# Pooled attention and a feed-forward block on one core: first values pooled by TensorE, five early tiles in float32, some weight shifts on GpSimd, and a new order of the first two chunks

## The chip, the cores and the metric

One core of a Trainium2 chip runs the whole program. The metric is the device time of one execution in microseconds; several executions are timed and the median is given. Engines are named as in the profile: PE (TensorE), PEld (its weight loads), DVE (VectorE), ACT (ScalarE), POOL (GpSimd), SP (the queue that issues nearly all DMAs).

## The reference

```
# q, k, v: [8 batches, 8 heads, 576, 64] float32
k_p = k.reshape(B, H, 72, 8, D).mean(axis=3)          # keys and values pooled by 8
v_p = v.reshape(B, H, 72, 8, D).mean(axis=3)
attn = softmax(q @ k_p^T / 8);  x = attn @ v_p         # -> x: [8, 576, 512]
xn = (x - mean) / sqrt(var + 1e-6) * g_ln              # layer norm over 512
out = x + relu(xn @ w_ch1) @ w_ch2                     # 512 -> 2048 -> 512
```

The two weight matrices arrive as float64 (8 MB each). q, k and v are float32.

## The kernel before

The 4608 rows are 36 tiles of 128, and nine chunks of four tiles. A batch is 576 rows, four and a half tiles, so that some tiles span two batches.

Attention of a tile t has two parts. `stage_a` (token A) loads a later tile's queries, computes the scores on PE in float32 against the pooled keys `kblk` (two buffers, one per batch in turn), subtracts the maximum on DVE, takes the exponential on ACT (`probs`), and brings the probabilities into a form with the keys on the partitions, `pt`. `values` (token B) multiplies by the pooled values, divides by the sum, computes the layer norm, and writes `zT`, the normalized tile transposed, as a float16 high and a float16 low half. For tiles below `XT` (8) the transposes are PE matmuls with an identity, and the split of `pt` into high and low halves is an ACT copy (L311) and a DVE subtract (L312); `values` then takes three float16 matmuls per head (L354). From tile 8 on the halves are made in SBUF on ACT and POOL (L314 to L324), and an SP DMA transposes them (L331, and L416 for z). Those tiles read the values in the split and doubled forms `VA` and `VB`, which ACT's queue copies.

The feed-forward of a chunk c is in three float16 products each way. `ffn_in` (L433) makes the hidden rows, 16 blocks of 128; token I.c.q is a quarter of them, with a third number for half of the columns. The result leaves PSUM by an ACT relu (L441) and a DVE subtract (L442) into a `ring` buffer. `ffn_out` (L462) makes the output rows in two halves of the hidden dimension; token O.c.h is half h for the four tiles. In full a chunk takes 192 matmuls of 512 columns each way.

The weights need work before any of this. Each of 8 blocks of 1 MB a matrix is loaded (token R.mat.b, `load_raw`) into a `raw` buffer (two of them) or, for the first four of w1, a `ring` buffer (four). `convert` (token C.mat.b) makes float32 of float64 by bits: ACT takes the high word (L165), DVE shifts the low word right by 29 (L168) and joins them (L169), and ACT's Abs pass (L177) sums magnitudes. After four blocks, `max_w1` or `max_w2` (M1.h, M2.h) derives a power-of-two scale over all partitions, and `split_w` (S.mat.b) writes the float16 halves, the high one on ACT (L140), the low one on DVE (L141).

Keys and values of later batches are loaded and pooled by adds on POOL (HK.b.i, HV.b.i: halves of a batch; the second HV also does `max_v` and `split_v`). For batch 0, `first_loads` (LD), `first_k` (K0) and `first_v` (V0) do it on DVE and POOL in turns; V0 ends in `max_v` and `split_v`.

The program of the first two chunks is the string `START`, a list of these tokens. It gives instructions their priority; the framework places them on the engines by a simulated timeline, so that an engine's order can differ from the list where an operand or a buffer isn't ready. On the chip each engine runs its own order and waits by semaphores. From chunk 2 on a loop writes the order: the 16 `ffn_in` and 8 `ffn_out` units of a chunk with `stage_a` and `values` of the next chunk between them.

Of the kernel before, what the change touches and what calls it, by code (L numbers as in the profile page):

```python
# [60 lines left out]
def attn_ffn_kernel(ctx: ExitStack, tc: tile.TileContext, qT, kT, v, g, w1, w2, out):  # L61
# [89 lines left out]
    def load_raw(mat, b):  # L151

        raw = ring_tile() if mat == 1 and b < NKT else raw_tile()
        raws[mat, b] = raw = raw.rearrange("p a f c -> p (a f c)").bitcast(I32)
        queue = nc.sync
        queue.dma_start(out=raw, in_=(w1, w2)[mat - 1][b].bitcast(I32))

    def convert(mat, b):
# [6 lines left out]
        nc.scalar.activation(  # L165
            out=w, in_=hi.bitcast(F32), func=AF.Prelu, scale=2.0**-112, alpha=-(2.0**32)
        )
        nc.vector.tensor_single_scalar(out=lo, in_=lo, scalar=29, op=ALU.logical_shift_right)  # L168
        nc.vector.scalar_tensor_tensor(  # L169
            out=w.bitcast(I32),  # L170
            in0=w.bitcast(I32),
            scalar=3,
            in1=lo,
            op0=ALU.logical_shift_left,
            op1=ALU.bitwise_or,
        )
        nc.scalar.activation(  # L177
            out=lo.bitcast(F32), in_=w, func=AF.Abs, accum_out=wm[mat][:, b : b + 1]
        )
# [48 lines left out]
    def pool_v(b, h, eng):  # L228
        if h == 0:
            vp[b] = wk1.tile([KV, H, D], F32, name="vp")  # L230
        vr = vraw.pop((b, h))
        eng.tensor_add(out=vr[:, 0:4, :], in0=vr[:, 0:4, :], in1=vr[:, 4:8, :])  # L232
# [1 line left out]
        eng.tensor_add(out=vp[b][:, h, :], in0=vr[:, 0, :], in1=vr[:, 1, :])  # L234

    def max_v(b):
        m = scalar_tile("mv")
        nc.vector.tensor_reduce(
            out=m[:KV], in_=vp[b], axis=AX.XY, op=ALU.max, apply_absolute_value=True
        )  # L240
# [59 lines left out]
    def probs(t):  # L300
        e, ph = E.pop(t), phl[t % 2]
        nc.scalar.activation(out=e, in_=e, func=AF.Exp, scale=EXP_SCALE)  # L302
        if t < XT:
# [7 lines left out]
            nc.scalar.copy(out=hi, in_=src)  # L311
            nc.vector.tensor_tensor(out=pt[:KV, H:], in0=src, in1=hi, op=ALU.subtract)  # L312
            return
# [19 lines left out]
    def values(t):  # L333

        segs = segments(t)
        if len(segs) == 1:
# [27 lines left out]
        nc.vector.tensor_scalar_mul(out=rs, in0=rs, scalar1=cv)
# [34 lines left out]
        nc.vector.tensor_scalar(  # L399
            out=z, in0=x, scalar1=mv[:, 0:1], scalar2=y, op0=ALU.subtract, op1=ALU.mult  # L400
        )
# [191 lines left out]
```

## Time and profile before

| | |
|---|---|
| Median of 3 runs | 910.19 us (909.65 to 911.42) |
| Span of the profiled execution | 911.2 us, the only time of its own that the page gives; 1.0 above the median |
| PE busy | 841.9 us, 92% |
| DVE busy | 442.5 us, 49% |
| ACT busy | 262.7 us, 29% |
| POOL busy | 237.6 us, 26% |
| Mean granted TensorE clock | 0.972 |
| HBM read, written | 45.09 MB, 9.44 MB |

The page's busy shares are for the whole span. Its forty slices are 22.8 us each, with a digit for tenths of busy time. An idle engine costs only where another waits for it. A row by line gives the line of the kernel, the engine, the operation, the tiles, shape and count, then the total busy time, the mean in ns, and the idle time before it with what ended that.

### The profile page before, as it was taken

The numbers are of one execution on the slowest core, as the hardware profiler recorded it, in microseconds if no ns is written. First come the engines' busy times: TensorE is split into PE (matmuls) and PEld (weight loads), VectorE is DVE, ScalarE is ACT, GpSimd is POOL, SyncE is SP. The second block draws the span as 40 slices with busy tenths as digits, with TensorE's granted clock in tenths as the row PEclk, the third lists the DMA queues.
The fourth block names the chain that finished last, engine by engine and source line by source line (L and its number), as shares of the span: only waits on it lengthen the run. The fifth ranks groups of instructions, "written<-read, shape, count | busy, mean of one in ns | idle before, by whom it ended". The sixth has DMA issues, their size and how long they took to land.

```text
span 911.2 us, 12223 instructions
## 1 busy us (share of the span) xinstructions
PE 841.9 (92%) x4692; PEld 433.7 (48%) x4692; DVE 442.5 (49%) x1038; ACT 262.7 (29%) x506; POOL 237.6 (26%) x390
## 2 busy tenths in 40 slices
PE   2433799999999999999999999999999999999998
PEld 1433685444454444455444544544454445444443
DVE  7978784336273555246424552553254335432121
ACT  2666551315132223132313321231223123211020
POOL 4874423004222761046101630131012001200000
PEclk9965799999999999999999999999999999999999
DMA  8867312103043542335222532233222221310001
GB/s 309 282 224 283 114 44 74 24 1 80 26 116 91 136 117 48 92 99 117 59 70 47 136 71 71 47 91 70 58 59 55 62 59 35 59 46 24 0 1 47
DMA packets 112010, 78.39 MB, mean 86 GB/s; under 512 B 90976, under 2 KB 91984, under 8 KB 109904
## 3 DMA queue, kind: packets, MB, share of 16 engines
q1 hardware_dynamic: 110608, 76.57, 31.2%
q10 hardware_dynamic: 1344, 1.05, 0.5%
q8 instruction: 37, 0.61, 0.3%
q14 instruction: 21, 0.17, 0.1%
HBM read 45.09 MB, written 9.44 MB: 60 GB/s over the span
## 4 chain that ended last, share of the span: by engine, by line
PE 81%; DMA 7%; POOL 5%; DVE 4%; issue 1%; ACT 1%; SPq 0%; POOLq 0%; DVEq 0%; ACTq 0%
PE ps_f L433 38%; PE ps_f L462 37%; DMA kr<-in_kT_dram 3%; PE ps L283 3%; POOL vr L232 2%; DMA raw<-in_w_dram 1%; DMA pt<-phl 1%; POOL kr L218 1%; DMA vr<-in_v_dram 1%; PE ps L356 1%; POOL vr L233 1%; PE ps L357 1%; POOL vp L234 1%; DMA raw<-in_v_dram 1%; DVE w L169 1%
## 5 line engine op out<-in xcount | busy, mean ns | idle before, releaser
L433 PE MATMUL ps_f<-zT,w 128*128 128x512 f16 (+1 forms) x1824 | 384.0, 369 | 0.0
L462 PE MATMUL ps_f<-w,ring 128*128 128x512 f16 x1728 | 378.9, 379 | 0.6 <-DVE ring L442 0.6
L433 PEld LDWEIGHTS <-w 128*128 128x128 f16 x1824 | 177.6, 98 | 187.5 <-issue 0.4
L462 PEld LDWEIGHTS <-ring 128*128 128x128 f16 x1728 | 168.3, 98 | 200.3 <-DVE ring L442 1.1
L442 DVE SCALAR_TENSOR_TENSOR ring<-ps_f,ring 128x512 f16<-128x512 f32 (+1 forms) x152 | 99.8, 659 | 142.6 <-ACT ring L441 139.1
L441 ACT ACTIVATE ring<-ps_f 128x512 f16<-128x512 f32 (+1 forms) x152 | 86.9, 574 | 249.1 <-PE ps_f L433 229.1
L472 DVE SCALAR_TENSOR_TENSOR x<-ps_f,c_out,x 128x512 f32<-128x512 f32 x72 | 53.9, 748 | 196.8 <-PE ps_f L462 192.4
L321 POOL TENSOR_TENSOR phl<-e,phl 128x512 f16<-128x512 f32 x28 | 32.8, 1170 | 252.1 <-ACT phl L314 237.4
L302 ACT ACTIVATE e<-e 128x576 f32<-128x576 f32 x36 | 24.6, 683 | 160.5 <-DVE e L293 151.4
L283 PE MATMUL ps<-kblk,q 128*128 128x144 f32 (+1 forms) x320 | 50.4, 322 | 20.3 <-ACT x L373 9.3
L415 POOL TENSOR_TENSOR hl<-z,hl 128x512 f16<-128x512 f32 x28 | 32.4, 1157 | 115.0 <-ACT hl L414 113.2
L373 ACT ACTIVATE x<-ps,rs 128x64 f32<-128x64 f32 x144 | 33.3, 315 | 100.2 <-DVE x L366 66.5
L283 PEld LDWEIGHTS ps<-kblk,q 128*128 128x128 f32 (+1 forms) x320 | 45.0, 203 | 28.9 <-ACT x L373 9.6
L232 POOL TENSOR_TENSOR vr<-vr 72x256 f32<-72x256 f32 x56 | 44.2, 795 | 34.4 <-DMA vr<-in_v_dram 34.2
L234 POOL TENSOR_TENSOR vp<-vr 72x64 f32<-72x64 f32 x56 | 20.4, 378 | 72.1 <-DVE vb L141 71.7
L218 POOL TENSOR_TENSOR kr<-kr 128x288 f32<-128x288 f32 x29 | 27.9, 966 | 43.2 <-DMA kr<-in_kT_dram 42.8
L377 DVE BATCH_NORM_STATS2 st<-x 128x6 f32<-128x512 f32 x36 | 24.9, 691 | 24.5 <-ACT x L373 24.4
L222 POOL TENSOR_TENSOR kblk<-kr 64x72 f32<-64x72 f32 x58 | 21.1, 364 | 48.3 <-PE ps L283 45.4
L414 ACT CAST hl<-z 128x512 f16<-128x512 f32 x28 | 17.3, 618 | 50.7 <-DVE z L399 47.2
L399 DVE TENSOR_SCALAR z<-x,mv,y 128x512 f32<-128x512 f32 x36 | 30.0, 834 | 2.8 <-DVE y L395 0.5
L292 DVE TENSOR_REDUCE mx<-ps 128x8 f32<-128x576 f32 x36 | 27.0, 750 | 5.0 <-PE ps L283 4.9
L314 ACT CAST phl<-e 128x1024 f16<-128x1024 f32 x28 | 29.2, 1042 | 0.5
(93 smaller groups left out, 539.0 us busy)
## 6 DMA issues: line engine op xcount, KB each, us to landing
raw<-in_w_dram SPq DMA_DIRECT2D x12, 1024.0 KB
q<-in_qT_dram SPq DMA_DIRECT2D x36, 256.0 KB
out_dram<-x SPq DMA_DIRECT2D x36, 256.0 KB
kr<-in_kT_dram SPq DMA_DIRECT2D x30, 288.0 KB
vr<-in_v_dram SPq DMA_DIRECT2D x56, 144.0 KB
ring<-in_w_dram SPq DMA_DIRECT2D x4, 1024.0 KB
raw<-in_v_dram SPq DMA_DIRECT2D x8, 144.0 KB
va<-vh ACTq DMA_DIRECT2D x14, 65.0 KB
```

What stands on the lines that cost most here:

```text
L218: eng.tensor_add(out=kr[:, 0:4, :], in0=kr[:, 0:4, :], in1=kr[:, 4:8, :])
L232: eng.tensor_add(out=vr[:, 0:4, :], in0=vr[:, 0:4, :], in1=vr[:, 4:8, :])
L283: nc.tensor.matmul(ps[r, p // 2, p % 2 * 2 * KV : (p % 2 + 1) * 2 * KV], lhsT=q[:, p, r], rhs=kblk[b % NKB][:, p, :], start=True, stop=True,)
L321: nc.gpsimd.tensor_tensor(out=ph[:, 0, :, KA:P], in0=e[:, :, 0:KA], in1=ph[:, 0, :, 0:KA], op=ALU.subtract)
L373: nc.scalar.activation(out=xh[:, 4 + i, :], in_=px[:, 1, i, 0:D], func=AF.Copy, scale=rs[:, 4 + i : 5 + i])
L399: nc.vector.tensor_scalar(out=z, in0=x, scalar1=mv[:, 0:1], scalar2=y, op0=ALU.subtract, op1=ALU.mult)
L415: nc.gpsimd.tensor_tensor(out=zhl[:, 1, :], in0=z, in1=zhl[:, 0, :], op=ALU.subtract)
L433: nc.tensor.matmul(ps, lhsT=w[:, part, fs], rhs=zT[:, kz, cols], start=(n == 0), stop=(n == 3 * NKT - 1),)
L441: nc.scalar.activation(out=h[:, 0, i, cols], in_=ps, func=AF.Relu)
L442: nc.vector.scalar_tensor_tensor(out=h[:, 1, i, cols], in0=ps, scalar=0.0, in1=h[:, 0, i, cols], op0=ALU.max, op1=ALU.subtract,)
L462: nc.tensor.matmul(ps, lhsT=h[:, part, i, cols], rhs=w[:, wp, j], start=(n == 0), stop=(n == 3 * NFT // 2 - 1),)
L472: nc.vector.scalar_tensor_tensor(out=x, in0=ps, scalar=c_out[:, half : half + 1], in1=x, op0=ALU.mult, op1=ALU.add)
```

## The change

- `XT` goes from 8 to 5. Tiles 0 to 4 keep the PE transposes, but `pt` stays float32 (one ACT copy, no subtract), and `values` takes one float32 matmul per head against the pooled values `vp` in float32, with a column of 8 for the sums. Their z is made by ACT instead of DVE. Tiles 5 to 7 take the path with DMA transposes.
- Batch 0's values are loaded as rows (a new input `vn`, token LV) and summed by groups of eight rows by five PE matmuls against a 0/1 matrix `pool_w`, which POOL builds at the start. Batch 0 has no `max_v` and `split_v` any more. Batch 0's keys are pooled three pairs on DVE and one on POOL.
- `convert` gets a flag; with it (a third number 1 in the C token) the shift of the low word is done by POOL, on its upper 16 bits. Ten of the sixteen blocks have it.
- `raw` gets a third buffer, `vp` a second. w1's first four blocks alone use the `ring`. The loads at the start are separate tokens (LK, Q, G, LV).
- `START` is written anew. The quarter I.0.1 of tiles 0 and 1 comes after the splits of w1's first four blocks and B.0 and B.1; I.0.3 and I.0.2 come ahead of O.0.0.

```diff
-XT = 8
+XT = 5
+FIRST_Q = 4
+RAW_RING = {(1, b) for b in range(4)}
 START = """
-LD K0 V0 R.1.0 A.0 R.1.1 B.0 R.1.2 A.1 B.1 R.1.3 C.1.3 C.1.0 C.1.2 A.2 A.3 R.2.0 C.1.1 HK.1.0 HK.1.1
-HV.1.0 M1.0 R.2.1 S.1.0 B.2 S.1.1 B.3 HV.1.1 A.4 S.1.2 A.5 C.2.1 S.1.3 I.0.0.0 R.1.4 C.2.0 B.4 A.6
-R.2.2 I.0.1.0 B.5 I.0.1.1 C.2.2 B.6 R.2.3 C.2.3 C.1.4 M2.0 R.2.4 S.2.0 R.1.5 R.1.6 S.2.1 A.7 I.0.0.1
-C.1.6 R.1.7 S.2.2 S.2.3 C.1.5 O.0.0 HK.2.0 B.7 I.1.1 I.1.0 C.1.7 M1.1 S.1.4 O.1.0 R.2.5 S.1.5 S.1.6
-R.2.6 S.1.7 R.2.7 C.2.4 A.8 I.0.2 C.2.5 HK.2.1 C.2.6 HV.2.0 B.8 C.2.7 A.9 M2.1 S.2.4 S.2.5 HV.2.1
-A.10 S.2.6 I.0.3 B.9 HK.3.0 I.1.2 S.2.7 HK.3.1 A.11 B.10 I.1.3 B.11 O.1.1 HV.3.0 O.0.1 HV.3.1
+LK K0 Q.0 R.1.2 Q.1 G R.1.7 LV R.2.6 R.1.0 C.1.0.1 R.2.4 R.1.1 C.1.1.1 V0 C.1.2 R.1.5 Q.2 HK.1.0
+R.1.6 A.0 A.1 R.1.3 R.2.0 C.2.0.1 R.1.4 HV.1.0 C.1.3.1 C.1.4.1 M1.0 S.1.0 R.2.1 S.1.1 B.0 C.2.6.1
+Q.3 S.1.2 B.1 C.1.6.1 R.2.3 A.2 S.1.3 R.2.2 I.0.1.0 C.1.7.1 A.3 R.2.5 C.1.5 B.2 B.3 C.2.2 M1.1
+HV.1.1 I.0.0.0 HK.1.1 I.0.1.1 S.1.4 C.2.1.1 A.4 A.5 C.2.4 I.0.0.1 C.2.5 S.1.5 A.6 C.2.3 S.1.6 S.1.7
+I.0.3 M2.0 A.7 R.2.7 C.2.7.1 B.4 S.2.0 S.2.1 B.5 A.8 S.2.2 HK.2.0 HV.2.0 M2.1 S.2.3 B.6 HK.2.1 S.2.4
+I.0.2 B.7 S.2.5 B.8 S.2.6 O.0.0 HV.2.1 S.2.7 O.0.1 A.9 I.1.1 I.1.3 HV.3.0 B.9 HK.3.0 I.1.0 A.10 B.10
+O.1.0 A.11 B.11 HV.3.1 I.1.2 HK.3.1 O.1.1
 """
...
-    rawp = ctx.enter_context(tc.tile_pool(name="rawp", bufs=2))
+    rawp = ctx.enter_context(tc.tile_pool(name="rawp", bufs=3))
...
-    def convert(mat, b):
+    def convert(mat, b, on_pool=0):
...
-        nc.vector.tensor_single_scalar(out=lo, in_=lo, scalar=29, op=ALU.logical_shift_right)
+        if on_pool:
+            top = raw.bitcast(U16).rearrange("p n (w u) -> p n w u", u=2)[:, :, 0, 1]
+            nc.gpsimd.tensor_scalar(
+                out=lo, in0=top, scalar1=2.0**-13, scalar2=2.0**-14 - 0.5, op0=ALU.mult, op1=ALU.add
+            )
+        else:
+            nc.vector.tensor_single_scalar(out=lo, in_=lo, scalar=29, op=ALU.logical_shift_right)
...
-            PT[t] = pt = wk2.tile([P, 2 * H, P], F16, name="pt")
-            hi, src = pt[:KV, 0:H], ps[:KV].rearrange("p a (h n) -> p (a h) n", n=P)
-            nc.scalar.copy(out=hi, in_=src)
-            nc.vector.tensor_tensor(out=pt[:KV, H:], in0=src, in1=hi, op=ALU.subtract)
+            nc.scalar.copy(out=pt[:KV], in_=ps[:KV])
...
-                    vl = VB[b][:KV, h, :]
-                    hi, lo = pt[:KV, h, r], pt[:KV, H + h, r]
-                    for n, (w, m) in enumerate(((hi, VH[b][:, h, :]), (hi, vl), (lo, VH[b][:, h, :]))):
-                        nc.tensor.matmul(o, lhsT=w, rhs=m, start=(n == 0), stop=(n == 2))
+                    nc.tensor.matmul(o, lhsT=pt[:KV, h, r], rhs=vp[b][:, h, :], start=True, stop=True)
...
-        nc.vector.tensor_scalar_mul(out=rs, in0=rs, scalar1=cv)
+        if cv:
+            nc.vector.tensor_scalar_mul(out=rs, in0=rs, scalar1=cv)
...
+        if t < XT:
+            nb = scalar_tile("nb")
+            nc.vector.tensor_scalar(
+                out=nb, in0=mv[:, 0:1], scalar1=y, scalar2=-1.0, op0=ALU.mult, op1=ALU.mult
             )
+            nc.scalar.activation(out=z, in_=x, func=AF.Identity, scale=y, bias=nb)
+        else:
+            nc.vector.tensor_scalar(
+                out=z, in0=x, scalar1=mv[:, 0:1], scalar2=y, op0=ALU.subtract, op1=ALU.mult
             )
...
     def first_k():
-        for p in range(NPAIR):
-            pool_k(0, p, (nc.vector, nc.gpsimd)[p % 2])
+        pool_k(0, 3, nc.gpsimd)
+        for p in range(3):
+            pool_k(0, p, nc.vector)
 
     def first_v():
-        for i in range(H):
-            pool_v(0, i, (nc.vector, nc.gpsimd)[i % 2])
-        max_v(0)
-        split_v(0)
+        ps = ps_f.tile([P, CH], F32, name="ps_f")[:KV]
+        rows = stage.pop("v")
+        for i, (x, w) in enumerate(rows):
+            nc.tensor.matmul(ps, lhsT=w, rhs=x, start=(i == 0), stop=(i == NRT - 1))
+        vp[0] = wk2.tile([KV, H, D + 1], F32, name="vp")
+        nc.vector.memset(vp[0][:, :, D:], float(POOL))
+        nc.scalar.copy(out=vp[0][:, :, 0:D], in_=ps.rearrange("p (h d) -> p h d", d=D))
```

More of the change, by code (lines that the diff above doesn't have):

```diff
@@ L12 @@
 I32 = mybir.dt.int32
+U16 = mybir.dt.uint16
 AF = mybir.ActivationFunctionType
@@ L40 @@
 NKB = 2
-XT = 8
+XT = 5
+FIRST_Q = 4
+NRT = -(-S // P)
 A_AT, B_AT = (0, 6, 10, 14), (5, 9, 13, 19)
@@ L60, in attn_ffn_kernel @@
 @with_exitstack
-def attn_ffn_kernel(ctx: ExitStack, tc: tile.TileContext, qT, kT, v, g, w1, w2, out):
+def attn_ffn_kernel(ctx: ExitStack, tc: tile.TileContext, qT, vn, kT, v, g, w1, w2, out):
     nc = tc.nc
@@ L88, in attn_ffn_kernel @@
     phl = [const.tile([P, 2, H, P], F16, name=f"phl{i}") for i in range(2)]
+    pool_w = const.tile([P, 2 * D + P // POOL], F32, name="pool_w")
+    ones = pool_w[:, D : D + P // POOL]
+    nc.gpsimd.memset(pool_w, 0.0)
+    nc.gpsimd.memset(ones, 1.0)
+    nc.gpsimd.affine_select(
+        out=ones, in_=ones, compare_op=ALU.is_ge, fill=0.0, base=0,
+        pattern=[[-POOL, P // POOL]], channel_multiplier=1,
+    )
+    nc.gpsimd.affine_select(
+        out=ones, in_=ones, compare_op=ALU.is_ge, fill=0.0, base=POOL - 1,
+        pattern=[[POOL, P // POOL]], channel_multiplier=-1,
+    )
     for t in kblk:
@@ L151, in load_raw @@
     def load_raw(mat, b):
-        raw = ring_tile() if mat == 1 and b < NKT else raw_tile()
+        raw = ring_tile() if (mat, b) in RAW_RING else raw_tile()
         raws[mat, b] = raw = raw.rearrange("p a f c -> p (a f c)").bitcast(I32)
@@ L229, in pool_v @@
         if h == 0:
-            vp[b] = wk1.tile([KV, H, D], F32, name="vp")
+            vp[b] = wk2.tile([KV, H, D + 1], F32, name="vp")
+            if b == 1:
+                nc.vector.memset(vp[b][:, :, D:], float(POOL))
         vr = vraw.pop((b, h))
@@ L238, in max_v @@
         nc.vector.tensor_reduce(
-            out=m[:KV], in_=vp[b], axis=AX.XY, op=ALU.max, apply_absolute_value=True
+            out=m[:KV], in_=vp[b][:, :, 0:D], axis=AX.XY, op=ALU.max, apply_absolute_value=True
         )
@@ L379, in values, with rsqrt @@
+    def rsqrt(var):
         ve, y, a = scalar_tile("ve"), scalar_tile("y"), scalar_tile("a")
         nc.vector.tensor_scalar(
-            out=ve, in0=mv[:, 1:2], scalar1=1e-6, scalar2=Z_VAR, op0=ALU.add, op1=ALU.mult
+            out=ve, in0=var, scalar1=1e-6, scalar2=Z_VAR, op0=ALU.add, op1=ALU.mult
         )
@@ L521, in first_k, with load_rows @@
-    def first_k():
-        for p in range(NPAIR):
-            pool_k(0, p, (nc.vector, nc.gpsimd)[p % 2])
-    def first_v():
-        for i in range(H):
-            pool_v(0, i, (nc.vector, nc.gpsimd)[i % 2])
-        max_v(0)
-        split_v(0)
+    stage = {}
+    def load_rows(name, src):
+        full = (NRT - 1) * P
+        a = raw_tile().rearrange("p a f c -> p (a f c)").bitcast(F32)
+        a = a.rearrange("p (r d) -> p r d", d=DM)
+        rest = wk2.tile([P, POOL, KV], F32, name="kr").rearrange("p l k -> p (l k)")[: S - full, :DM]
+        nc.sync.dma_start(out=a, in_=src[:full].rearrange("(r p) d -> p r d", p=P))
+        nc.sync.dma_start(out=rest, in_=src[full:])
+        stage[name] = [(a[:, r], pool_w[:, D - r * P // POOL :][:, :KV]) for r in range(NRT - 1)]
+        r = NRT - 1
+        stage[name].append((rest, pool_w[: S - full, D - r * P // POOL :][:, :KV]))
```

135 lines of the change are left out of this document (68 added, 67 removed).

## The prediction

> **What bounds the kernel now.** I read the forty slices of the page first, then the busy time by stage, then the timeline around the two places where the feed-forward matmuls begin, and last the costs by line.
>
> ```profile
> PE 841.9 (92%) x4692; PEld 433.7 (48%) x4692; DVE 442.5 (49%) x1038; ACT 262.7 (29%) x506; POOL 237.6 (26%) x390
> PE   2433799999999999999999999999999999999998
> DVE  7978784336273555246424552553254335432121
> PEclk9965799999999999999999999999999999999999
> ```
> ```profile
> 0.00:90.00 90.00, 32.37 (x209) 26.60 (x210) 75.08 (x165) 50.06 (x76) 55.43 (x91) 0.80 0.79 273
> 0.00:133.50 133.50, 70.57 (x579) 59.98 (x580) 110.68 (x266) 73.84 (x128) 70.11 (x119) 0.81 0.62 212
> 133.50:911.00 777.50, 771.33 (x4115) 373.71 (x4113) 331.81 (x773) 188.84 (x379) 167.47 (x272) 1.00 0.27 64
> ```
> ```profile
> 88.25 1.02 DVE L399 TENSOR_SCALAR z<-x,mv,y 128x512 f32<-128x512 f32 x1
> 90.31 2.75 PE L433 MATMUL ps_f<-zT,w 128*128 128x256 f16 x12
> ...
> 133.40 0.38 PE L462 MATMUL ps_f<-w,ring 128*128 128x512 f16 x1
> ```
> ```profile
> 199.32 10.36 PE ps_f L433 x48
> ```
>
> The columns of the second fence are the stretch, its length, then busy time of PE, weight loads, DVE, ACT and POOL, clock, DMA share and GB/s. The reader is to see two kernels in one. From 133.5 us on PE is busy 771.3 of 777.5 us: whatever is done there by other engines is hidden. Before it DVE is the busiest, 75.1 of 90 us and 110.7 of 133.5, both 83%. The first feed-forward matmul stands at 90.31, behind the z of tile 3 at 88.25; the first of the second product (O.0.0) at 133.40.
>
> A quarter of the first product (48 matmuls, one I token) takes 10.36 us. At 133.4 only I.0.0 and I.0.1 were done, 20.7 us of work. So PE stands 133.4 - 20.7 = 112.7 us behind a PE that had done nothing but feed-forward from the start. I call this the lag. After 133.5 nothing is saved or lost, since the attention of tile 9 onwards and all later chunks stay as they are (each tile's scores are a microsecond of PE, below). So the new time is 911.2 less what the lag shrinks by.
>
> **The change, part by part.** The costs of DVE, ACT, POOL and PE in the first 200 us, by line and shape:
>
> ```profile
> L169 DVE SCALAR_TENSOR_TENSOR w<-w,raw 128x1024 int32<-128x1024 int32 x12 | 14.9, 1245 | 0.6 <-ACT w L165 0.6
> L165 ACT ACTIVATE w<-raw 128x1024 f32<-128x1024 f32 x12 | 13.8, 1151 | 9.5 <-DMA raw<-in_w_dram 9.5
> L177 ACT ACTIVATE raw<-w 128x1024 f32<-128x1024 f32 x12 | 13.6, 1131 | 5.4 <-DVE w L169 5.4
> L141 DVE SCALAR_TENSOR_TENSOR w<-w,gs 128x1024 f16<-128x1024 f32 x8 | 11.1, 1384 | 3.1 <-ACT w L140 3.0
> L312 DVE TENSOR_TENSOR pt<-ps,pt 72x1024 f16<-72x1024 f32 x8 | 9.7, 1218 | 0.5 <-ACT pt L311 0.5
> L168 DVE TENSOR_SCALAR raw<-raw 128x1024 int32<-128x1024 int32 x12 | 9.2, 770 | 7.9 <-DMA raw<-in_w_dram 7.9
> L140 ACT ACTIVATE w<-w,gs 128x1024 f16<-128x1024 f32 x8 | 9.2, 1148 | 7.4 <-DVE w L141 7.1 <-DVE gs L189 0.2
> L442 DVE SCALAR_TENSOR_TENSOR ring<-ps_f,ring 128x512 f16<-128x512 f32 x8 | 5.5, 691 | 13.0 <-ACT ring L441 13.0
> L411 DVE TENSOR_TENSOR zT<-ps_f,zT 128x512 f16<-128x512 f32 x8 | 5.5, 682 | 0.0
> L399 DVE TENSOR_SCALAR z<-x,mv,y 128x512 f32<-128x512 f32 x8 | 5.1, 635 | 0.2 <-PE ps_f L409 0.2
> L410 ACT CAST zT<-ps_f 128x512 f16<-128x512 f32 x8 | 4.7, 587 | 19.4 <-PE ps_f L409 19.3
> L364 DVE TENSOR_SCALAR rs<-rs,cv 128x8 f32<-128x8 f32 x8 | 2.9, 361 | 0.1
> L321 POOL TENSOR_TENSOR phl<-e,phl 128x512 f16<-128x512 f32 x2 | 2.3, 1154 | 12.4 <-ACT phl L314 12.3
> L234 DVE TENSOR_TENSOR vp<-raw 72x64 f32<-72x64 f32 x4 | 2.2, 557 | 0.0
> L232 DVE TENSOR_TENSOR raw<-raw 72x256 f32<-72x256 f32 x4 | 2.2, 548 | 1.5 <-DMA raw<-in_v_dram 1.5
> L238 DVE TENSOR_REDUCE mv<-vp 72x1 f32<-72x512 f32 x3 | 2.0, 679 | 0.5 <-POOL vp L234 0.5
> L141 DVE SCALAR_TENSOR_TENSOR vb<-vp,sv,vh 72x512 f16<-72x512 f32 x2 | 1.5, 748 | 0.0
> L222 DVE TENSOR_TENSOR kblk<-ring 64x72 f32<-64x72 f32 x2 | 1.0, 476 | 0.0
> ```
>
> What DVE loses ahead of O.0.0:
> - Batch 0's values (V0): four heads of three adds at some 0.55 us, 6.6, and max and split, 0.68 + 0.75: 8.0 us. They become five float32 matmuls and an ACT copy.
> - No low half of the probabilities (L312): in all of the first eight tiles, 8 x 1.218 = 9.7. Tiles 0 to 4 stay in float32; tiles 5 to 7 go the way of tiles 8 onwards, whose subtracts are on POOL.
> - z on ACT in five tiles: 5 x 0.635, less one short DVE instruction each, which I put at 0.15 (an estimate, as the short ones here): 2.4. No multiplication by cv: 5 x 0.361 = 1.8. No L411 in tiles 5 and 6 (tile 7's fell after the mark): 1.4.
> - Ten shifts on POOL: 10 x 0.770 = 7.7.
> - One more pair of keys on DVE: +1.5 by L222 twice and two more adds of about a quarter microsecond each.
>
> Together -29.5. The order brings forward four splits of w1's second half (4 x 1.384) and I.0.2 and I.0.3 with eight evictions (8 x 0.691): +11.0. Net -18.5 as a sum of rows. Rows overlap, so I take 0.88 of it (my estimate: what all of DVE's rows up to 133.5 give, some 126 us, against 110.7 busy): -16.3, which leaves 94.4 busy. At the old 83% O.0.0 starts at 114.
>
> What goes elsewhere. ACT: five z at the price of L410's 0.587 to a conversion's half of 1.15 (I take 0.65, nearest the 512-wide row), four splits of 1.148, eight evictions of about 0.6: 73.8 + 13 = 87 in 114 us, 76%; it stays second. POOL: ten shifts of 1024 elements that the trace doesn't have. By operands read, L321's 1.154 us for 2 x 512 gives 1.2 us; by elements 2.3. I take 1.2, since a shift has one input; 12 to 23 us in all. Tiles 5 to 7 bring about 2.7 each. POOL's 70.1 loses 6 from V0 and ends near 90 of 114 at most.
>
> PE, whose idle hides these costs until the first feed-forward:
>
> ```profile
> 23.53 2.26 PE L283 MATMUL ps<-kblk,q 128*128 128x144 f32 x8
> ...
> 255.54 1.14 PE L283 MATMUL ps<-kblk,q 128*128 128x144 f32 x8
> ```
>
> Four score matmuls are eight float32 passes, 0.28 us each early on and 0.14 late. Pooling the values is ten passes of 512 columns: 5 to 10 us. Eight float32 value matmuls are sixteen passes of 65 columns with full weight loads, 2.0 (by columns) to 4.5 us (by passes) a tile early on. Neither is on the path if the weights come later.
>
> The first feed-forward. Its new needs are R.1.3, two tiles and four splits.
>
> ```profile
> raw<-in_w_dram SPq DMA_DIRECT2D x12, 1024.0 KB
> q<-in_qT_dram SPq DMA_DIRECT2D x36, 256.0 KB
> kr<-in_kT_dram SPq DMA_DIRECT2D x30, 288.0 KB
> ```
>
> Batch 0's keys (1.2 MB) and values (1.2), three query tiles, R.1.2, R.1.7, R.1.0, R.1.1, R.1.3, and maybe R.2.6 and half of batch 1's keys, are 8.3 to 10.0 MB on SP's queue; at the 273 GB/s of the first 90 us they land at 31 to 37. Convert (1.15 + 1.25 + 1.13 and waits), max and four splits: 43 to 50, where it was 90.3. Values: keys, two query tiles and two blocks stand ahead of them, so they land near 20, are pooled at 30, and B.0 and B.1 end near 40. From 47 to 114 PE has 41.4 us of I and about 17 of attention: it fits, with little to spare. The three raw buffers let SP run further ahead, but R.1.7, R.2.6 and R.2.4 hold them early; q, key and transpose issues that stand behind a load waiting for a buffer wait with it. B.5 to B.7, the first tiles with a transpose on SP, are not needed before chunk 1, 20.7 us after O.0.0 starts, and that covers a stall of 10 us.
>
> A longer DVE instruction beside POOL:
>
> ```profile
> L141 DVE SCALAR_TENSOR_TENSOR w<-w,gs x4: 1267/1458/1751, 59.5 to 71.8; 128x1024 f16<-128x1024 f32 x4
> L141 DVE SCALAR_TENSOR_TENSOR w<-w,ws x2: 1273/1274/1274, 130.9 to 133.4; 128x1024 f16<-128x1024 f32 x2
> ...
> L169 DVE SCALAR_TENSOR_TENSOR w<-w,raw x12: 1185/1214/1536, 35.2 to 103.6; 128x1024 int32<-128x1024 int32 x12
> ```
> ```profile
> 60.00:70.00 10.00, 1.48 (x24) 1.31 (x23) 9.51 (x16) 5.89 (x7) 6.78 (x6) 0.50 0.42 149
> 120.00:133.00 13.00, 13.00 (x138) 11.91 (x137) 10.02 (x27) 7.44 (x16) 0.67 (x2) 1.00 0.09 24
> ```
>
> The split is 14% longer (1458 against 1274 ns) where POOL is busy 6.8 of 10 us than where it is idle; L169's median is not. On 12 more us of POOL that is 1 to 2 us of DVE; I add 1. The Trainium skill ("GPSIMD Engine Reference", Specifications) says that POOL shares its SBUF interfaces with VectorE and contends with DVE instructions that have two SBUF inputs; L141 bears that out and L169's median hardly. If all of DVE's remaining two-input work, some 35 us, paid the 14%, it would be 5 us, and the time 876.
>
> **Sum.** O.0.0 at 115 with four quarters done, 41.4 us: lag 73.6, which is 39.1 less than 112.7. 911.2 - 39.1 = 872 in the profiled execution, whose span is 1.0 above the median of 910.19: 871.
>
> **The rivals.**
> - PE is fed all the way: DVE waits less than before, since loads come earlier. First matmul at 47, then nothing but I and about 14 us of attention: lag 61, time 858. Against it: DVE's 94 us must be at its end by 102.
> - PE is cold. Scores cost 2.26 us at 23.53 and 1.14 at 255.54, though the page's clock says 9 in both. If all that PE does from 47 on in pieces runs at half speed, I.0.0 and I.0.1 take 41 and the attention 25, up to 113, and the other two quarters 20.7 more: lag 92.5, time 890. Against it: once busy without a gap PE gets fast (12 matmuls in 2.75 at 90.31). The Trainium skill ("TensorE: Matmul & The Clock Gate", Part 1) says that idling for some 3.4 us halves the clock and as long a busy stretch restores it; the durations agree, the clock column does not.
> - The loads come late: SP stands at a raw block whose buffer is held, and R.1.3 behind it. If the first matmul stays at 90, DVE's saving still lets all four quarters run through, with about 8 us of attention between: lag 98, time 896.
> - Slower: the shift on POOL takes many times the 1.2 us. Eight of them stand ahead of w1's second maximum, behind at most 55 us of other POOL work. That is no loss until S.1.7 passes 133, so from (127 - 55)/8 = 9 us a shift; each us above it costs 8. At 10 us: 918. Against it: POOL's dearest row above is 1.154 us.
> - It does nothing: the planner places instructions by its own times, and the order written is only a priority. Then 910.
>
> **How the numbers follow.** Forecast 0.58, with 862 to 884 (83% busy read as 90% and 75%); fed 0.14; cold 0.10; loads late 0.08; slower 0.07; nothing 0.03. Faster by over 0.2% (about what a measurement here can tell from no change) is 0.90, within it 0.03, slower 0.07. From 856 to 897 leaves out the last two cases.
>
> **What would show it.** Right: the first feed-forward matmul at 43 to 50, O.0.0 near 115 with I.0.2 and I.0.3 ahead of it, DVE about 94 us busy until then, POOL's shift at 1.2 to 2.3 us, PE without a gap from there to the end. Wrong: PE idle by several us after O.0.0; a shift of many us; PE's halves at 0.23 us each up to I.0.3; a raw load that waits on SP while DVE is idle.

## The result, and the profile after

The changed kernel takes 876.96 us (median of 4 runs, 876.73 to 877.38), the kernel before 910.70 beside it: ratio 0.9626, 95% interval 0.9611 to 0.964. The forecast was 871. The profiled execution has a span of 875.4 us.

Busy times of the changed kernel and PE's forty slices, as in the view of before (a slice is 21.9 us now):

```profile
PE 840.3 (96%) x4593; PEld 427.2 (49%) x4593; DVE 423.4 (48%) x995; ACT 264.3 (30%) x514; POOL 257.4 (29%) x397
...
PE   5669899999999999999999999999999999999998
```

The five slices ahead of PE's unbroken nines read 5 6 6 9 8 instead of 2 4 3 3 7. PE is busy for nearly as long as before (840.3 against 841.9 us), so the difference is idle time at the start.

The stages of the changed kernel (stretch, length, busy PE, weight loads, DVE, ACT, POOL, clock, DMA share, GB/s) and the places on PE that bound them (start, length, engine, line, tiles, count, idle before and what ended it):

```profile
47.20:123.00 75.80, 63.85 (x458) 42.78 (x459) 72.84 (x158) 54.52 (x101) 73.03 (x104) 0.88 0.73 210
60.00:123.00 63.00, 55.55 (x407) 37.28 (x408) 61.62 (x133) 45.74 (x87) 60.44 (x89) 0.90 0.72 195
0.00:123.00 123.00, 92.09 (x604) 64.80 (x605) 106.45 (x242) 86.32 (x151) 98.55 (x145) 0.89 0.82 261
123.00:875.40 752.40, 748.21 (x3994) 362.42 (x3990) 316.99 (x754) 178.02 (x364) 158.81 (x253) 1.00 0.27 65
```
```profile
47.20 2.76 PE L466 MATMUL ps_f<-zT,w 128*128 128x256 f16 x12
...
97.54 8.81 PE L466 MATMUL ps_f<-zT,w 128*128 128x512 f16 x40
...
108.84 0.20 PE L399 MATMUL ps<-va,pt 128*128 128x65 f16 x1 [1.97 <-DMA pt<-phl]
...
110.40 12.21 PE L466 MATMUL ps_f<-zT,w 128*128 128x512 f16 x48
122.96 20.88 PE L495 MATMUL ps_f<-w,ring 128*128 128x512 f16 x96
```

L466 is `ffn_in` in the new file, L495 `ffn_out`. The first feed-forward matmul stands at 47.20 (90.31 before) and O.0.0 at 122.96 (133.40), with I.0.3 at 97.54 and I.0.2 at 110.40 ahead of it. So the lag is 123.0 - 41.4 = 81.5 us, 31.2 less than before. The span fell by 35.8. The other 4.6 us lie almost wholly after O.0.0: there PE is idle for 4.2 us (6.2 before), and it has 2.4 us less to do beside the two quarters that moved ahead (771.3 - 20.7 = 750.6 against 748.2).

Between 60 and 123 us DVE is busy for 61.6 of 63 us and POOL for 60.4. At first sight DVE is the bound. The experiments show that this is only half true: work added to DVE costs time, and work taken from it gains none.

### The profile page after: what moved, and what is told of

Read it like the earlier page. It is cut to its first block, busy times and chain, and to the rows that moved or that the text cites. A ratio compares the mean times of both kernels' runs of the same rounds, so it can differ in the third digit from the quotient of the medians.

```text
span 875.4 us, 12018 instructions
## 1 busy us (share of the span) xinstructions
PE 840.3 (96%) x4593; PEld 427.2 (49%) x4593; DVE 423.4 (48%) x995; ACT 264.3 (30%) x514; POOL 257.4 (29%) x397
## 4 chain that ended last, share of the span: by engine, by line
PE 83%; DMA 7%; POOL 6%; DVE 2%; issue 1%; SPq 1%; POOLq 0%
PE ps_f L495 40%; PE ps_f L466 38%; PE ps L307 3%; DMA kr<-in_kT_dram 2%; DMA ring<-in_w_dram 2%; POOL vr L257 1%; DMA vr<-in_v_dram 1%; POOL kr L241 1%; DMA raw<-in_w_dram 1%; PE ps L399 1%; PE ps L400 1%; POOL kblk L245 1%; POOL vr L258 1%; POOL raw L187 1%; POOL kr L242 1%
## 5 line engine op out<-in xcount | busy, mean ns | idle before, releaser
L466 PE MATMUL ps_f<-zT,w 128*128 128x512 f16 (+1 forms) x1824 | 388.0, 371 | 5.9 <-DVE y L360 3.4
L495 PE MATMUL ps_f<-w,ring 128*128 128x512 f16 x1728 | 378.2, 379 | 0.0
L466 PEld LDWEIGHTS <-w 128*128 128x128 f16 x1824 | 177.9, 99 | 196.3 <-DVE w L158 4.8
L495 PEld LDWEIGHTS <-ring 128*128 128x128 f16 x1728 | 168.2, 98 | 200.2 <-issue 0.2
L342 POOL TENSOR_TENSOR phl<-e,phl 128x512 f16<-128x512 f32 x31 | 36.2, 1168 | 273.7 <-ACT phl L335 261.4
L448 POOL TENSOR_TENSOR hl<-z,hl 128x512 f16<-128x512 f32 x31 | 36.1, 1164 | 128.5 <-ACT hl L447 122.4
L307 PE MATMUL ps<-kblk,q 128*128 128x144 f32 (+1 forms) x320 | 47.4, 311 | 9.9 <-DMA q<-in_qT_dram 7.5
L257 POOL TENSOR_TENSOR vr<-vr 72x256 f32<-72x256 f32 x56 | 46.6, 841 | 17.0 <-DMA vr<-in_v_dram 16.4
L245 POOL TENSOR_TENSOR kblk<-kr 64x72 f32<-64x72 f32 x58 | 25.0, 431 | 43.9 <-PE ps L307 40.7
L258 POOL TENSOR_TENSOR vr<-vr 72x128 f32<-72x128 f32 x56 | 33.3, 606 | 0.8
L335 ACT CAST phl<-e 128x1024 f16<-128x1024 f32 x31 | 32.3, 1041 | 0.5
L369 DVE SCALAR_TENSOR_TENSOR a<-y,ve 128x1 f32<-128x1 f32 x108 | 29.8, 278 | 2.9
L432 DVE TENSOR_SCALAR z<-x,mv,y 128x512 f32<-128x512 f32 x31 | 27.4, 883 | 5.2 <-POOL hl L448 2.9
```

The source lines that it names most:

```text
L245: eng.tensor_add(out=kblk[b % NKB][r, p, c], in0=kr[r, 0, :], in1=kr[r, 1, :])
L307: nc.tensor.matmul(ps[r, p // 2, p % 2 * 2 * KV : (p % 2 + 1) * 2 * KV], lhsT=q[:, p, r], rhs=kblk[b % NKB][:, p, :], start=True, stop=True,)
L342: nc.gpsimd.tensor_tensor(out=ph[:, 0, :, KA:P], in0=e[:, :, 0:KA], in1=ph[:, 0, :, 0:KA], op=ALU.subtract)
L448: nc.gpsimd.tensor_tensor(out=zhl[:, 1, :], in0=z, in1=zhl[:, 0, :], op=ALU.subtract)
L466: nc.tensor.matmul(ps, lhsT=w[:, part, fs], rhs=zT[:, kz, cols], start=(n == 0), stop=(n == 3 * NKT - 1),)
L495: nc.tensor.matmul(ps, lhsT=h[:, part, i, cols], rhs=w[:, wp, j], start=(n == 0), stop=(n == 3 * NFT // 2 - 1),)
```

## The experiments

Each kernel was timed in three rounds beside the kernel before. "First" is the first feed-forward matmul, the lag is O.0.0 less the feed-forward work done until then, and the last column is the span less the lag.

| kernel | ratio to before (95%) | median, us | first | O.0.0 | lag | rest |
|---|---|---|---|---|---|---|
| before | 1 | 910.7 | 90.3 | 133.4 | 112.7 | 798.5 |
| the change | 0.9626 (0.9611 to 0.964) | 877.0 | 47.2 | 123.0 | 81.5 | 793.9 |
| shifts on DVE | 0.9738 (0.9722 to 0.9755) | 887.9 | 49.9 | 133.1 | 91.6 | 794.6 |
| POOL light | 0.961 (0.9596 to 0.9624) | 875.9 | 47.3 | 123.2 | 81.8 | 792.3 |
| old order | 1.0055 (1.0035 to 1.0075) | 917.0 | 84.0 | 114.6 | 93.9 | 818.1 |
| old arithmetic | 1.0297 (1.0277 to 1.0316) | 938.0 | 65.2 | 184.6 | 143.2 | 793.3 |
| eight float32 tiles | 0.9936 (0.9912 to 0.9959) | 905.6 | 46.8 | 152.8 | 111.4 | 792.4 |
| old order, eight float32 tiles | 0.9964 (0.9951 to 0.9977) | 908.4 | 84.3 | 129.8 | 109.1 | 797.5 |
| values added on DVE and POOL | 0.9744 (0.9721 to 0.9767) | 888.8 | 51.5 | 135.5 | 94.1 | 793.5 |
| I.0.2 early | 0.9665 (0.9638 to 0.9692) | 880.8 | 48.8 | 124.2 | 82.8 | 795.3 |
| later B tokens | 0.9608 (0.959 to 0.9626) | 876.9 | 47.2 | 121.3 | 79.8 | 794.6 |
| all shifts on POOL | 0.9657 (0.9641 to 0.9673) | 880.9 | 45.0 | 124.9 | 83.5 | 794.9 |
| z on ACT | 0.9616 (0.9598 to 0.9634) | 877.3 | 47.2 | 122.9 | 81.5 | 795.8 |
| all reliefs | 0.9604 (0.9576 to 0.9632) | 876.1 | 45.2 | 122.5 | 81.1 | 792.9 |

The rest is 792 to 796 in every kernel with the new order, over lags from 80 to 143. So the lag does carry the time. The one exception, 818 in the old order, is looked at below.

**Shifts on DVE.** All sixteen shifts stay on DVE.

```diff
-C.1.0.1 ... C.1.1.1 ... C.2.0.1 ... C.1.3.1 C.1.4.1 ...
+C.1.0 ... C.1.1 ... C.2.0 ... C.1.3 C.1.4 ...
```

> The changed kernel with all sixteen weight shifts on DVE. Theory W (DVE's own work ahead of O.0.0 sets the time): ten shifts of 0.69 to 0.97 us come back to DVE, 7 to 8 us as rows, so O.0.0 moves from 123 to about 130 and the time is 882 to 885. Rival N (what POOL is given it takes from DVE by lengthening DVE's instructions): POOL loses 12 us of work, DVE's splits get shorter again, and the time stays at 875 to 879.

Its span is 886.2, 10.8 us over the change's, and O.0.0 is 10.1 later. The time, 887.9, is 3 us above the range of theory W. DVE's shifts in its first 133 us, and what PE waited for most (total, times, longest):

```profile
L191 DVE TENSOR_SCALAR raw<-raw 128x1024 int32<-128x1024 int32 x12 | 12.1, 1008 | 0.1
```
```profile
PE ps L332 <- ACT e L326: 17.9, 4, 6.2
```

The shift takes 1008 ns here, not the 770 of before, so ten are about 10 us: in this order they cost their full length. PE pays while it waits for exponentials (L332 are the transposes of the probabilities), which come after DVE's maximum and subtraction of the same tile.

**Values of batch 0 added on DVE and POOL**, from eight loads, as before; no max and no split.

```diff
     def first_v():
-        ... matmuls with pool_w into ps_f, an ACT copy
+        for i in range(H):
+            pool_v(0, i, (nc.vector, nc.gpsimd)[i % 2])
+        nc.vector.memset(vp[0][:, :, D:], float(POOL))
```

> The changed kernel with batch 0's values added on DVE and POOL from eight loads, in place of PE's pooling (no split of them either). Theory W: 6.6 us of DVE come back, and the time is 882 to 885. Rival H (they come back in the first 30 us, where DVE is busy 20 of 30 and waits for weights): time 876 to 880.

Span 887.6: 12.2 us slower than the change, for adds that take 8.1 us on DVE here and 7.7 on POOL, not the expected 6.6. Neither range held (888.8). That this part might be hidden is wrong. The adds stand at the very start of the order, and everything moves back with them: the first feed-forward by 4.3, O.0.0 by 12.6.

**Old order with the new arithmetic.** `START` as before, with ten of its C tokens marked for POOL and the new load tokens in place of LD; two queries loaded first.

```diff
-LK K0 Q.0 R.1.2 Q.1 G R.1.7 LV R.2.6 R.1.0 C.1.0.1 ...
+Q.0 LK LV Q.1 G K0 V0 R.1.0 A.0 R.1.1 B.0 ...          (the old list)
-FIRST_Q = 4
+FIRST_Q = 2
```

> The new arithmetic (five float32 tiles, values pooled on PE, ten shifts on POOL, three raw buffers) with the old order of the first chunks. Theory W: DVE has some 25 us less to do before O.0.0 than before the change, O.0.0 stands near 105 with two quarters done, lag 84, time 880 to 886. Rival O (the order makes the gain, since it feeds PE early and puts four quarters ahead of O.0.0): time 897 to 906.

917 us: slower than before and outside both ranges, though O.0.0 stands at 114.6, earlier than in any other kernel here. By the lag alone (93.9) it should gain 19 us. The stages of this kernel, what PE waited for after 114 us, and the timeline of one tile show where they went:

```profile
114.60:140.00 25.40, 21.76 (x94) 9.44 (x93) 11.54 (x21) 5.89 (x9) 8.70 (x13) 0.93 0.29 66
140.00:160.00 20.00, 7.71 (x59) 5.56 (x58) 9.33 (x24) 3.80 (x9) 10.33 (x19) 0.67 0.51 125
```
```profile
PE ps L398 <- DMA pt<-phl: 12.3, 1, 12.3
```
```profile
141.33 1.22 PE L306 MATMUL ps<-kblk,q 128*128 128x144 f32 x8
...
144.36 0.68 ACT L325 ACTIVATE e<-e 128x576 f32<-128x576 f32 x1 [0.53 <-DVE e L316]
145.07 1.04 ACT L334 CAST phl<-e 128x1024 f16<-128x1024 f32 x1
...
148.50 1.33 POOL L341 TENSOR_TENSOR phl<-e,phl 128x512 f16<-128x512 f32 x1
...
150.13 1.76 SPq L351 DMA_TRANSPOSE pt<-phl  x1
...
154.84 0.24 PE L398 MATMUL ps<-va,pt 128*128 128x65 f16 x1 [12.29 <-DMA pt<-phl]
```

This is tile 8: the ninth set of scores on PE, and the fourth tile that an SP DMA transposes. Its scores are on PE at 141.3 and its probabilities are back, transposed, at 154.8: 13.5 us by way of DVE, ACT, POOL and a DMA, and nothing else stands in PE's order between them. Tile 8 goes this way in the kernel before too. There PE does most of its scores at the start of O.0.0, which covers the way (PE's timeline of the kernel before):

```profile
133.62 0.90 PE L283 MATMUL ps<-kblk,q 128*128 128x144 f32 x6
134.35 20.67 PE L462 MATMUL ps_f<-w,ring 128*128 128x512 f16 x95
```

With five float32 tiles the framework put them behind O.0.0; why is not shown.

**Old order with eight float32 tiles** takes that wait away (`XT = 8`; everything else as in the kernel above).

> The new arithmetic in the old order, with eight float32 tiles: tiles 5 to 7 don't take the DMA transpose. Theory L: the old order with five float32 tiles lost 12.3 us after O.0.0 in one wait for a transposed tile 7; that wait goes, and the time is 895 to 904. Rival O (the old order can't use the new arithmetic at all): the wait is replaced by one for z or w1's second half at the same place, time 908 to 917.

PE is busy for 770.8 of the 776.2 us after the mark, so the 12.3 us are gone (they were tile 8's, not tile 7's): tile 8's scores stand at 124.3, ahead of O.0.0. But the first product starts at 84, and the lag is 109.1. The time, 908.4, is 0.36% under before. So the new arithmetic alone is worth next to nothing in the old order, whichever way tiles 5 to 7 go.

**Old arithmetic in the new order.** Eight tiles with split probabilities, batch 0's values from adds with max and split, two pairs of its keys each on DVE and POOL, shifts and z on DVE; B.4 and B.5 stand ahead of A.6 and A.7.

```diff
-XT = 5
+XT = 8
-            nc.scalar.copy(out=pt[:KV], in_=ps[:KV])
+            nc.scalar.copy(out=hi, in_=src)
+            nc.vector.tensor_tensor(out=pt[:KV, H:], in0=src, in1=hi, op=ALU.subtract)
...
```

> The old arithmetic (eight early tiles with splits, values of batch 0 added on DVE and POOL, all shifts on DVE, z on DVE, two pairs of keys each on DVE and POOL) with the new order and three raw buffers; B.4 and B.5 stand two tiles earlier in the list, since eight tiles need the buffers. Theory W: DVE has 26 us more to do ahead of O.0.0 than in the changed kernel, O.0.0 near 145 to 150, time 898 to 906. Rival O: time 880 to 888.

The worst of all, 938 us: 3% slower than before and far outside both ranges. What PE waited for most until O.0.0:

```profile
PE ps L330 <- ACT e L326: 31.1, 6, 11.5
PE ps_f L446 <- DVE z L436: 14.6, 4, 6.2
PE ps L403 <- DMA pt<-phl: 11.1, 1, 11.1
```

With the old arithmetic, the order that puts four quarters ahead of O.0.0 is a loss. Order alone +3.0%, arithmetic alone +0.6% (-0.4% with eight float32 tiles), both together -3.7%: the two parts do not add. But this "order alone" also holds the eight tiles with their two moved tokens, and the next run shows that with the new arithmetic these cost 28 of the 61 us between this kernel and the change.

**Eight float32 tiles in the new order**: only the tiles 5 to 7 change (`XT = 8`, B.4 and B.5 moved as above).

> The changed kernel with eight float32 tiles instead of five (tiles 5 to 7 transposed by PE again, without splits), B.4 and B.5 two tiles earlier in the list as eight such tiles need their buffers. Theory L (the new order works because tiles 5 to 7 leave PE and ACT and have time for the longer way through POOL and the DMA transpose): PE gets 3 us more a tile ahead of O.0.0, and the two moved tokens hold others up, time 884 to 895. Rival S (only the missing splits matter, 1.2 us of DVE a tile): time 874 to 880.

Span 903.8, 28.4 us more than with five; the time, 905.6, is outside both ranges. PE waits for exponentials for 11.9 us, and again 10.0 at once for a transposed tile (tile 8):

```profile
PE ps L332 <- ACT e L326: 11.9, 3, 5.2
PE ps L399 <- DMA pt<-phl: 10.0, 1, 10.0
```

Five is thus no detail of the change. How much of the 28 us is the number of tiles and how much the two moved tokens, this run cannot say.

**POOL light.** The pooling of later batches on POOL leaves out two of its three adds, to see what POOL's load does to DVE.

```diff
-        eng.tensor_add(out=kr[:, 0:4, :], ...)
-        eng.tensor_add(out=kr[:, 0:2, :], ...)
+        if b == 0: (the same two adds)
-        eng.tensor_add(out=vr[:, 0:4, :], ...)
-        eng.tensor_add(out=vr[:, 0:2, :], ...)
```

> The changed kernel in which POOL's pooling of the later batches leaves out two of its three steps of adds (keys and values of batches 1 to 7 are then not the pooled ones). Some 45 us less POOL work ahead of O.0.0. Theory N (a busy POOL lengthens DVE's instructions): the split of w1's blocks, 1626 ns on average in the changed kernel, goes back to 1270 to 1400, O.0.0 comes 6 to 10 us earlier, time 866 to 871. Theory W alone (DVE's work sets the time and POOL doesn't touch it): durations stay, time 874 to 877. Rival Q (POOL's queue itself delays tiles 5 to 8): durations stay, but B.6 and B.7 come earlier, time 872 to 875.

Some of DVE's dearest shapes in the first 123 us, first of the changed kernel, then of this one, and then this kernel's window from 60 to 123:

```profile
L192 DVE SCALAR_TENSOR_TENSOR w<-w,raw 128x1024 int32<-128x1024 int32 x12 | 16.3, 1360 | 3.8 <-ACT w L182 2.4 <-POOL raw L187 1.5
L158 DVE SCALAR_TENSOR_TENSOR w<-w,gs 128x1024 f16<-128x1024 f32 x8 | 13.0, 1626 | 0.0
L372 DVE SCALAR_TENSOR_TENSOR y<-a,y 128x1 f32<-128x1 f32 x18 | 6.1, 340 | 0.1
L191 DVE TENSOR_SCALAR raw<-raw 128x1024 int32<-128x1024 int32 x5 | 4.9, 972 | 0.0
```
```profile
L192 DVE SCALAR_TENSOR_TENSOR w<-w,raw 128x1024 int32<-128x1024 int32 x12 | 15.9, 1323 | 2.7 <-ACT w L182 2.6
L158 DVE SCALAR_TENSOR_TENSOR w<-w,gs 128x1024 f16<-128x1024 f32 x8 | 10.2, 1274 | 0.0
L371 DVE SCALAR_TENSOR_TENSOR y<-a,y 128x1 f32<-128x1 f32 x24 | 5.6, 233 | 0.1
L191 DVE TENSOR_SCALAR raw<-raw 128x1024 int32<-128x1024 int32 x5 | 3.6, 711 | 0.0
```
```profile
60.00:123.00 63.00, 53.97 (x404) 37.91 (x405) 54.32 (x158) 45.60 (x88) 24.60 (x42) 0.92 0.74 203
```

With POOL busy for 24.6 us instead of 60.4, the split falls from 1626 to 1274 ns, the shift from 972 to 711, and DVE from 61.6 to 54.3 us busy, with more instructions done (158 against 133). So POOL stretches DVE, some instructions by much and others, as the join of the words (L192, 1360 to 1323), hardly. Yet O.0.0 stays at 123.2 and the interval of the time overlaps the change's. DVE's 98% was not what set the end: theory N is right on the durations and wrong on the time.

**Four more reliefs.** Each takes a different load off. z of tiles 5 to 8 on ACT:

```diff
-        if t < XT:
+        if t < 9:
             nb = scalar_tile("nb")
```

> The changed kernel with z on ACT for tiles 5 to 8 too, as for tiles 0 to 4. DVE loses three z of 0.73 us ahead of O.0.0, ACT gains three of 0.81. Theory W: 2 us, time 874 to 876. Rival C (ACT and DVE are chained instruction by instruction, and a step handed from one to the other gains nothing, as with POOL's relief of DVE): 876 to 880.

DVE 57.3 of the 63 us, O.0.0 at 122.9, the time the same. All sixteen shifts on POOL (third number 1 in every C token):

> The changed kernel with all sixteen weight shifts on POOL. Theory W: DVE loses six more shifts, 4 to 6 us, time 871 to 873, since ten of them were worth 11 us. Rival P (POOL, busy 96% of 60 to 123 us, now is as much on the path as DVE, and delays tiles 5 to 8): time 877 to 882.

0.9657, O.0.0 at 124.9: slightly slower than the change, whose interval ends where this one begins. The tokens B.5 to B.8 put later:

```diff
-S.2.1 B.5 A.8 S.2.2 HK.2.0 HV.2.0 M2.1 S.2.3 B.6 HK.2.1 S.2.4 I.0.2 B.7 S.2.5 B.8 S.2.6 O.0.0
+S.2.1 S.2.2 HK.2.0 HV.2.0 M2.1 S.2.3 S.2.4 I.0.2 O.0.0 B.5 A.8 S.2.5 B.6 HK.2.1 S.2.6 B.7 ... B.8
```

> The changed kernel with B.5, B.6, B.7 and A.8 moved in the list behind O.0.0, and w2's first splits and I.0.2 ahead of them. Theory W (DVE's work ahead of O.0.0 sets the time): DVE loses three values stages there, some 12 us, O.0.0 starts 8 to 11 us earlier and B.5 to B.7 are done under O.0.0 and O.0.1 (41 us); time 866 to 870. Rival F (the planner fills idle places with whatever is ready, so the engines' orders hardly change): within 2 us of the changed kernel, 875 to 879. Rival L (I.1.1 then waits for tile 7, as in the old order): 879 to 888.

On PE only tile 8's values moved, behind O.0.0; those of tiles 5 to 7 still stand ahead of I.0.2 (92.7, 107.2 and 109.8 us). O.0.0 comes 1.7 us earlier, but the time is 876.9, not to be told from the change. And I.0.2 right behind I.0.3:

```diff
-I.0.3 M2.0 A.7 ... I.0.2 B.7
+I.0.3 I.0.2 M2.0 A.7 ... B.7
```

> The changed kernel with I.0.2 moved in the list right behind I.0.3, ahead of M2.0 and B.4 to B.7. Theory T (PE stands in its own order for tile 7's transposed probabilities, 2 us at 107, and cools down, so that I.0.2 takes 12.2 us instead of 10.4): PE runs I.0.3 and I.0.2 in one piece, O.0.0 starts 2 to 4 us earlier, time 872 to 875. Rival D (DVE's work up to w2's splits sets O.0.0, and eight evictions ahead of it push it back): time 877 to 881.

880.8: w2's first high halves come late now, and O.0.0 itself waits for them (2.0 us, `PE ps_f L495 <- ACT w L157`). Theory T isn't tested by this: the wait for tile 7 (1.9 us) still stands ahead of I.0.2, which starts only 1.9 us earlier, at 108.5, and takes 12.4 us again.

**All reliefs at once**: POOL light (the same adds are left out), B later, z on ACT.

> The three reliefs of DVE together, none of which moved the time alone: POOL's pooling of the later batches without two of its three steps of adds (batches 1 to 7 are then not pooled as they should be), z on ACT for tiles 5 to 8, and B.5 to B.7 and A.8 behind O.0.0 in the list. Theory K (several bounds tie, and a relief that isn't for all of them gains nothing): with some 20 us less on DVE and 45 less on POOL, O.0.0 starts 6 to 12 us earlier, time 864 to 870. Rival E (PE's own order and the way from scores to transposed probabilities set O.0.0, whatever DVE does): 872 to 877.

O.0.0 at 122.5, 876.1 us: rival E's range, not theory K's. The window and what PE waits for in it:

```profile
60.00:123.00 63.00, 54.53 (x401) 37.56 (x400) 52.16 (x156) 46.39 (x89) 24.98 (x43) 0.90 0.80 206
```
```profile
PE ps L398 <- DMA pt<-phl: 4.0, 2, 2.7
PE ps_f L441 <- ACT z L429: 2.6, 1, 2.6
PE ps_f L441 <- DVE y L359: 1.4, 1, 1.4
```

DVE has 10.8 us of idle time in 63 and ACT 16.6, and PE is as busy as before (54.5 against 55.6). Most of what PE does up to O.0.0 is feed-forward. By line and shape, of the change and then of this kernel:

```profile
L466 PE MATMUL ps_f<-zT,w 128*128 128x256 f16 x192 | 26.0, 293 | 5.9 <-DVE y L360 3.4 <-DVE ring L475 1.0 <-ACT w L157 0.8
L466 PE MATMUL ps_f<-zT,w 128*128 128x512 f16 x96 | 22.9, 400 | 0.1
```
```profile
L465 PE MATMUL ps_f<-zT,w 128*128 128x256 f16 x192 | 25.6, 292 | 4.6 <-DVE w L158 3.5 <-ACT w L157 1.1
L465 PE MATMUL ps_f<-zT,w 128*128 128x512 f16 x96 | 22.5, 394 | 0.2 <-DVE ring L474 0.2
```

The four quarters take 48.9 us in the change and 48.1 here, where full speed is 41.4. Of the change's 75.8 us between the first feed-forward matmul and O.0.0, 48.9 are feed-forward, 15.0 attention and the like (63.85 - 48.9), and 12.0 idle. PE without any idle time would be at O.0.0 at 111, with its feed-forward at full speed too at 103.5. So between the change and a PE that is its own bound lie many short gaps (the longest wait above is 2.7 us) and slow matmuls. These are terms of a sum. That O.0.0 would come earlier with every matmul at full speed is not shown: in POOL light I.0.2 runs near full speed, in 10.5 us instead of 12.2, and so it does with z on ACT, but PE's idle time up to O.0.0 is 13.1 and 14.1 us there instead of 12.0, and O.0.0 stays. Only with later B tokens do the 1.7 us of a faster I.0.2 show in O.0.0.

```profile
112.84 10.52 PE L465 MATMUL ps_f<-zT,w 128*128 128x512 f16 x48 [0.18 <-DVE rowmax L123]
```

What stays open: why these gaps keep their sum when DVE, POOL and ACT are relieved. At one place the last kernel's trace shows it. I.0.3 ends there at 102.9 instead of 106.3, yet I.0.2 starts at 110.9 instead of 110.4. Between them PE now has a tile's scores (2.0 us) that stand elsewhere in the change, and waits 4.2 us instead of 2.0: for a transposed tile (2.7 us), then for DVE. DVE has itself stood idle for the maximum over batch 3's values, which the list has behind O.0.1 and the change does at 131.9, and POOL for their load:

```profile
106.92 0.32 POOL L258 TENSOR_TENSOR vp<-vr 72x64 f32<-72x64 f32 x1 [3.44 <-DMA vr<-in_v_dram]
108.11 0.68 DVE L262 TENSOR_REDUCE mv<-vp 72x1 f32<-72x512 f32 x1 [4.13 <-POOL vp L258]
```

So a relieved engine came to its next wait sooner, and another gap opened. Whether that holds for the rest, or a fixed chain through the splits or through SP's loads and transposes sets O.0.0, no run tells: none relieves SP's queue. No variant here is faster than the change beyond its interval.

## Why the prediction came out as it did

The time lies 6 us above the forecast, within its range. That it lies so near is partly luck: the lag shrank by 31.2 us instead of 39.1, and 4.6 us that the prediction had put at nothing were gained after O.0.0.

- **The lag as the measure: right.** Span less lag is 792 to 799 in every kernel but one. "After 133.5 nothing is saved or lost" missed 4.6 us, and it breaks where an order leaves PE nothing under the way of a transposed tile (818 in the old order, 20 us over before).
- **The first feed-forward at 43 to 50: right**, 47.2. So were four quarters ahead of O.0.0, and PE without a large gap after it (748.2 of 752.4).
- **O.0.0 at 115: 8 us late**, at 123.0. This is the step that missed. It has two parts. The term "+1" for DVE stretched beside POOL was mis-sized: taking each DVE group of one operation, tile and shape that both kernels have up to O.0.0, count by (mean after less mean before) adds up to 12.8 us, in POOL light to 0.5. DVE's rows up to O.0.0 add up to 122.1; less those 12.8 they are 109.3, against 126.3 - 18.5 = 107.8 by the prediction: the work taken away was counted about rightly, its new price was not. But the stretch isn't what made O.0.0 late, since O.0.0 stays at 123 without it. The 83% rule took DVE for the only bound. The sentence that should have been priced is "it fits, with little to spare": from the first matmul PE was given 41.4 + 17 us of 68; it took 48.9 + 15.0 and was idle for 12.0. As a sum, 7.5 of the 8 us are feed-forward at less than full speed, attention is 2.0 shorter, and the idle time is 2.4 longer than the 9.6 that were left. Which of them moved O.0.0 stays open, as said above.
- **Where the 7.5 come from.** The 48 matmuls of half width from 47.2 to 64.7 took 9.2 us (5.2 at full speed; clock 0.77 in 47 to 60, 0.53 in 60 to 70), and I.0.2, behind the gap at 106 to 110, took 12.2 for 10.4 (clock 0.86 from there to O.0.0). That is 5.8; the rest is spread. "PE is cold", the rival at 0.10, was thus partly at work: it put all of I.0.0 and I.0.1 at half speed, and only the pieces next to gaps were. The row that the prediction holds against it was misread: 12 matmuls of half width in 2.75 us at 90.31 are 0.23 us each, about half speed (10.36 us for a quarter make 0.108). The ones at full speed come behind them, 0.114 each:

```profile
95.42 4.10 PE L433 MATMUL ps_f<-zT,w 128*128 128x256 f16 x36
```

The stages of the change around the slow pieces, and the piece behind its longest wait:

```profile
47.20:60.00 12.80, 8.30 (x51) 5.50 (x51) 11.23 (x25) 8.78 (x16) 12.59 (x15) 0.77 0.81 287
60.00:70.00 10.00, 7.52 (x34) 5.33 (x34) 9.17 (x17) 7.71 (x15) 9.59 (x12) 0.53 0.53 184
...
106.20:110.40 4.20, 2.18 (x40) 1.76 (x38) 4.13 (x9) 2.81 (x7) 4.05 (x10) 1.00 0.45 100
110.40:123.00 12.60, 12.60 (x65) 5.63 (x65) 12.60 (x29) 7.57 (x16) 12.34 (x21) 0.86 0.67 157
```
```profile
58.93 0.78 PE L466 MATMUL ps_f<-zT,w 128*128 128x256 f16 x4 [3.38 <-DVE y L360]
```

The Trainium skill ("TensorE: Matmul & The Clock Gate", Part 1) has the clock fall after some 3.4 us of idling; the trace agrees for the piece behind the 3.38 us wait at 58.9, but the low clock from 110.4 on follows a stretch of 4.2 us in which PE was busy for 2.2 (the third row), and behind like stretches of 3.5 and 3.7 us in the runs with later B tokens and z on ACT it is 1.00.

- **POOL's shift at 1.2 us: right**, and so the rival of a slow shift is gone. z on ACT was put at 0.65 and takes 0.81; POOL was put at 90 of 114 at most and is busy for 98.6 of 123:

```profile
L187 POOL TENSOR_SCALAR raw<-raw 128x1024 int32<-128x1024 uint16 x7 | 8.8, 1257 | 9.8 <-DMA raw<-in_w_dram 9.3
L430 ACT ACTIVATE z<-x,nb,y 128x512 f32<-128x512 f32 x5 | 4.1, 814 | 0.4 <-DVE nb L427 0.4
```

- **Taking 0.88 of the rows for DVE's saving: too little.** Ten shifts were priced at 7.7 and are worth 10.8 us of span; the values' adds were priced at 6.6 (8.0 with max and split), and their return alone costs 12.2. Around this kernel, work added costs its measured length on DVE or more (10.1 us for 10.8, 8.1 for 12.2), and work taken away beyond it gains nothing.
- **The rivals.** PE fed all the way (858) did not come: the idle 12.0 us and the slow matmuls' 7.5 are 19.5 of the 20.5 by which the lag exceeds that rival's 61. Loads late did not come, by the first matmul at 47.2. That the written order does nothing is refuted by the old order's 917.

## What to carry to other kernels

An engine at 98% in a window need not be what sets the window's end. Before taking its saving as time, price the second engine's whole path through the window too, at the speed it has beside its gaps. Test an order and the arithmetic that it was written for together; either alone can lose. When an order is tight, look for the long way of one tile (scores to transposed probabilities, 13.5 us here) and make sure that work of that length stands under it.
